# Two value products in turn instead of interleaved, and later normalizations in batch 0, in an attention and gated-MLP kernel

## The chip, the cores and the metric

The kernel runs on one core of a Trainium2 chip. The metric is the device time of one execution in microseconds (us). An execution here is about 216 us; the span in a profile is some 1.8 us shorter. Its profile shows five engines: TensorE (PE, and PEld for its weight loads), VectorE (DVE), ScalarE (ACT), GpSimd (POOL) and SyncE (SP), which here issues transfers. They run side by side (the busy times of the first four add up to 275% of the span). Each has its own queue, which it works through in order, and the traces show what it waited for. To evict a product is to copy it out of its PSUM buffer, so that the buffer is free for the next product.

## The reference, cut to what matters

```python
# attention, 4 batches x 8 heads, 768 positions, head size 64, block-sparse mask
attn = softmax(where(mask, q @ k.T / 8, -1e9)) @ v        # -> x: (4, 768, 512)
# gated MLP per batch
h = relu(x @ w_in)                     # 512 -> 1024
u, v = h[..., :512], h[..., 512:]
v_n = (v - mean(v)) / sqrt(var(v) + 1e-6)
v_s = w_spatial @ v_n + b_spatial      # mixes the 768 positions
out = (u * v_s) @ w_out
```

The MLP of one batch runs on TensorE in the gaps of the attention of the next batch. The 768 positions are six chunks of 128. For each chunk there is a value product (v0 to v5), a gate product (u0 to u5), a spatial product (s0 to s5) and an output product (o0 to o5).

## The kernel before

TensorE's queue is a chain of steps, here called slots: two score matmuls, then one to three matmuls of the MLP ("units"), then six matmuls of the attention product. A batch has 108 units: 12 products of 4, then 6 of 6, then 6 of 4. The units are a list from which each slot takes a few. Every product takes one of two alternating PSUM buffers:

```python
def bank(shape, dtype):
    moe_bank[0] = 1 - moe_bank[0]
    return psum.tile(shape, dtype, tag=f"moe{moe_bank[0]}", bufs=1, name="ps_moe")
```

so a product can start only when the product before last has been evicted. A value product is evicted on VectorE with a ReLU (L543), then its mean and variance are taken (L546, L547); after every third chunk GpSimd computes three reciprocal deviations. The normalizations (L557) are put in a queue with a due time:

```python
def v_post(tcc, ps):
    ... # ReLU into vsb, bn_stats, bn_aggr into mv
    if tcc % 3 == 2:
        ... # std, rstd on nc.gpsimd
        norm_q.extend((i, 2 * products[0] + (6 if tcc == 2 else 3)) for i in range(tcc - 2, tcc + 1))
```

`normalize_next` is called in the middle of every product with the time `2 * products[0]` (products finished so far, doubled) and after every gate product with one more; it issues at most one normalization that is due. The order of the products, and the pairs whose matmuls alternate:

```python
order = ("v0 v1 u0 v2 u1 u2 v3 v4 u3 v5 u4 u5" if b == 0 else
         "v0 v1 v2 v3 v4 v5 u0 u1 u2 u3 u4 u5" if last else
         "v0 v1 u0 v2 u1 v3 u2 v4 u3 v5 u4 u5")
for n, (w, tcc) in enumerate(order.split()):
    ... # append the four units of this product
    if n == 1 and not last or b == 0 and n == 7:
        two = units[-2 * NDM:]
        units[-2 * NDM:] = [two[i % 2 * NDM + i // 2] for i in range(2 * NDM)]
```

Interleaving two products puts off the moment at which the last quarter of `xt` (the attention output, transposed) is needed: at the seventh unit instead of the fourth.

In the experiments three more numbers matter: in which step of a head pair the casts of q, k and v on GpSimd, their transposes and the next load are issued.

```python
s_prep = {NG: 7, NG + 1: 7}.get(p, 1)                                  # casts
s_tr = {NG: 10, NG + 1: 9}.get(p, 8 if change else 6)                  # transposes
s_load = {NG: 11, NG + 1: 10, NG + 3: 10}.get(p, 9 if change else 7)   # loads
```

The softmax here doesn't subtract the row's maximum and nothing guards it: scores larger than these inputs give would overflow.

Of the kernel before, what the change touches and what calls it, by code (L numbers as in the profile page):

```python
# [26 lines left out]
def kernel(  # L27
# [469 lines left out]
    def moe_units(b):  # L497
        last = b == B - 1
# [15 lines left out]
        norm_q = deque()  # L514
        products = [0]
# [23 lines left out]
        def v_post(tcc, ps):  # L539
            if last:  # L540
                nc.scalar.activation(out=vsb[:, tcc, :], in_=ps, func=AF.Relu)  # L541
            else:
                nc.vector.tensor_scalar(out=vsb[:, tcc, :], in0=ps, scalar1=0.0,  # L543
                                        scalar2=None, op0=ALU.max)
            stats = work.tile([128, 6], FP32, tag="stats", bufs=2)
            nc.vector.bn_stats(out=stats, in_=vsb[:, tcc, :])  # L546
            nc.vector.bn_aggr(out=mv[:, tcc, :], in_=stats)  # L547
            if tcc % 3 == 2:
                cs = slice(tcc - 2, tcc + 1)
                nc.gpsimd.tensor_scalar(out=std[:, cs], in0=mv[:, cs, 1], scalar1=1e-6,  # L550
                                        scalar2=None, op0=ALU.add)
                nc.gpsimd.tensor_tensor(out=rstd[:, cs], in0=std[:, cs],
                                        in1=mhalf[:, cs], op=ALU.pow)
                norm_q.extend((i, 2 * products[0] + (6 if tcc == 2 else 3)) for i in range(tcc - 2, tcc + 1))

        def normalize(tcc):
            nc.vector.tensor_scalar(out=vn[:, tcc, :], in0=vsb[:, tcc, :],  # L557
# [12 lines left out]
        def in_proj(tcc, cols, post):  # L570
            add(NDM, lambda g: (xt(g)[:, tcc * 128:(tcc + 1) * 128], w_in_t[:, g, cols]),
                lambda ps: post(tcc, ps))
# [4 lines left out]
        for n, (w, tcc) in enumerate(order.split()):  # L577
            if w == "v":
                in_proj(int(tcc), slice(DH, DFF), v_post)
            else:  # L580
                in_proj(int(tcc), slice(0, DH), u_post)
            if n == 1 and not last or b == 0 and n == 7:
                two = units[-2 * NDM:]
                units[-2 * NDM:] = [two[i % 2 * NDM + i // 2] for i in range(2 * NDM)]

# [108 lines left out]
    for g in range(N0):  # L694
# [27 lines left out]
        if g == 26:  # L722
            moe_q.extend(moe_units(0))
# [26 lines left out]
    for p in range(NG, NP + 1):  # L750
# [6 lines left out]
        for s in range(12):  # L757
# [40 lines left out]
            if s == 11 and change:  # L798
                if p == 2 * NG:
                    for third in range(3):  # L800
                        xtr_third(p - 1, third)
                moe_q.extend(moe_units(p // NG - 1))
                slots_left = 48 if p < NP - NG else 49
                budget = 0.0
    for _ in range(len(moe_q) // 2):
        moe_q.popleft()()
    xtr(NP - 1)
    moe_q.extend(moe_units(B - 1))
    while moe_q:
        moe_q.popleft()()  # L810
# [28 lines left out]
```

## Time and profile before

| | before |
|---|---|
| time, median (range), 6 runs | 216.11 us (215.44 to 216.28) |
| span of the profiled run | 214.0 us |
| busy: TensorE, ScalarE, VectorE, GpSimd | 96%, 80%, 66%, 32% |
| slots at the places that the change touches | see the slot table under the result |

A slot's length is the distance between the starts of two successive pairs of score matmuls (L371) in TensorE's timeline. Slots are numbered g = 48, 49, ... in the order of the program; g = 48 starts the second batch's attention. In an undisturbed slot one unit makes 0.74 us, two 0.95, three 1.17. A longer slot is a stall of TensorE or holds other work as well (slot 107, 1.29, has six transposes).

### The profile page before, as it was taken

How to read it: one execution, taken by the hardware profiler on the slowest of the kernel's cores; microseconds unless marked ns; L12 is line 12 of the kernel's file. 1: busy time of each engine (PE TensorE's matmuls, PEld its weight loads, DVE VectorE, ACT ScalarE, POOL GpSimd, SP SyncE). 2: the span in 40 equal slices, each digit the busy share in tenths (PEclk: the TensorE clock that was granted, in tenths of full speed). 3: DMA queues.
4: the chain of work that ended last, by engine and by line, in shares of the span. 5: the costliest groups of instructions: out<-in, count | busy, mean ns of one | idle time of the engine just before them, and what ended most of it. 6: DMA issues, size and time to landing. Idle time of an engine off the chain costs nothing.

```text
span 214.0 us, 5304 instructions
## 1 busy us (share of the span) xinstructions
PE 206.0 (96%) x2077; PEld 126.8 (59%) x2111; DVE 141.7 (66%) x361; ACT 172.1 (80%) x238; POOL 68.8 (32%) x97
## 2 busy tenths in 40 slices
PE   8999999998999999999999999999999999999993
PEld 7667766665666666655566556555656656544441
DVE  6877949859784746366979465367869544585542
ACT  7799999998999989988899888888899885266031
POOL 6768979801440704031515310401502000022000
PEclk9999999999999999999999999999999999999999
DMA  5999999978689997999788948989902124620246
GB/s 155 305 334 381 394 349 276 213 131 254 148 225 243 282 292 131 101 308 283 258 255 118 279 89 238 229 181 284 178 1 40 25 52 86 222 101 0 58 117 242
DMA packets 64136, 42.04 MB, mean 196 GB/s; under 512 B 46096, under 2 KB 59760, under 8 KB 64112
## 3 DMA queue, kind: packets, MB, share of 16 engines
q1 hardware_dynamic: 63824, 41.39, 76.1%
q8 instruction: 16, 0.26, 0.5%
q10 hardware_dynamic: 288, 0.33, 0.5%
q14 instruction: 8, 0.07, 0.1%
HBM read 24.38 MB, written 6.29 MB: 143 GB/s over the span
## 4 chain that ended last, share of the span: by engine, by line
PE 75%; DMA 9%; issue 6%; DVE 5%; POOL 2%; SPq 1%; ACT 1%; POOLq 0%; ACTq 0%; DVEq 0%
PE ps_moe L530 29%; PE ps L371 16%; PE ps_av L387 11%; PE ps L406 5%; PE ps_t L530 3%; DMA st_q<-in_q_dram 3%; PE ps_sc L530 3%; PE ps_av L422 2%; DMA tt_q<-nat_q 2%; DMA st_k<-in_k_dram 2%; PE wps L216 2%; DMA w_spt<-ws_nat 2%; POOL vv L143 1%; DVE osb L629 1%; DVE kt_all L280 1%
## 5 line engine op out<-in xcount | busy, mean ns | idle before, releaser
L375 ACT ACTIVATE a_all<-ps 128x768 bf16<-128x768 f32 x144 | 113.3, 813 | 15.2 <-PE ps L371 8.9
L371 PE MATMUL ps<-qt_all,kt_all 88*128 88x384 bf16 x288 | 70.3, 325 | 0.0
L387 PEld LDWEIGHTS <-a_all 128*128 128x128 bf16 x864 | 46.1, 97 | 34.5 <-issue 2.1
L387 PE MATMUL ps_av<-vv,a_all 128*128 128x65 bf16 x864 | 50.8, 194 | 0.4
L530 PE MATMUL ps_moe<-w_in_t,xt 128*128 128x512 bf16 x143 | 45.1, 378 | 1.5 <-DVE vsb L543 0.9
L410 ACT ACTIVATE a_all<-ps 128x768 bf16<-128x768 f32 x48 | 35.6, 812 | 2.1 <-PE ps L406 1.5
L140 POOL CAST nat_k<-st_k 128x768 bf16<-128x768 f32 (+1 forms) x14 | 10.9, 780 | 76.4 <-DMA st_k<-in_k_dram 59.5
L530 PE MATMUL ps_moe<-vn,w_spt 128*128 128x512 bf16 x109 | 33.0, 378 | 0.5
L530 PEld LDWEIGHTS <-xt 128*128 128x128 bf16 x192 | 18.6, 97 | 14.4 <-issue 0.2
L596 DVE SCALAR_TENSOR_TENSOR gn<-ps_moe,b_col,un 128x512 bf16<-128x512 f32 x20 | 15.0, 749 | 17.7 <-PE ps_moe L530 13.1
L406 PE MATMUL ps<-qt_all,kt_all 88*128 88x384 bf16 x96 | 23.4, 325 | 0.7 <-ACT a_all L410 0.2
L530 PE MATMUL ps_moe<-w_out_t,gt 128*128 128x512 bf16 x74 | 21.5, 378 | 0.2
L530 PEld LDWEIGHTS <-w_spt 128*128 128x128 bf16 x144 | 13.8, 97 | 11.6
L371 PEld LDWEIGHTS <-kt_all 88*128 88x128 bf16 x288 | 19.1, 98 | 0.5 <-issue 0.2
L422 PEld LDWEIGHTS <-a_all 128*128 128x128 bf16 x288 | 14.9, 98 | 5.9 <-issue 0.6
L543 DVE TENSOR_SCALAR vsb<-ps_moe 128x512 bf16<-128x512 f32 x18 | 12.3, 682 | 8.7 <-PE ps_moe L530 8.7
L546 DVE BATCH_NORM_STATS2 stats<-vsb 128x6 f32<-128x512 bf16 x24 | 16.6, 694 | 1.5 <-ACT vsb L541 0.8
L422 PE MATMUL ps_av<-vv,a_all 128*128 128x65 bf16 x288 | 17.0, 194 | 0.1
L550 POOL TENSOR_SCALAR std<-mv 128x3 f32<-128x3 f32 x8 | 1.9, 242 | 41.9 <-DVE mv L547 32.6
L360 DVE COPY qt_all<-tt_q 64x384 bf16<-64x384 bf16 x48 | 14.5, 339 | 0.5
L360 DVE COPY kt_all<-tt_k 64x384 bf16<-64x384 bf16 x48 | 14.4, 338 | 0.2
L629 DVE COPY osb<-ps_moe 128x512 f32<-128x512 f32 x10 | 6.9, 689 | 11.4 <-PE ps_moe L530 7.9
(106 smaller groups left out, 218.7 us busy)
## 6 DMA issues: line engine op xcount, KB each, us to landing
out_dram<-osb SPq DMA_DIRECT2D x23, 256.0 KB, 3.0
st_v<-in_v_dram SPq DMA_DIRECT2D x14, 384.0 KB, 5.4
st_k<-in_k_dram SPq DMA_DIRECT2D x13, 384.0 KB, 4.9
st_q<-in_q_dram SPq DMA_DIRECT2D x12, 384.0 KB, 3.7
wst<-in_moe_w_spatial_dram SPq DMA_DIRECT2D x3, 768.0 KB, 9.3
wst<-in_moe_w_in_dram SPq DMA_DIRECT2D x4, 512.0 KB, 7.5
wst<-in_moe_w_out_dram SPq DMA_DIRECT2D x2, 512.0 KB, 7.5
st_q<-in_q_dram SPq DMA_DIRECT2D x4, 192.0 KB, 6.1
```

The lines of the kernel that those rows point to most:

```text
L140: eng.tensor_copy(out=dst, in_=src)
L360: nc.vector.tensor_copy(out=dst[0:D, c * 128:(c + 3) * 128], in_=src[h * D:(h + 1) * D, c:c + 3, :])
L371: nc.tensor.matmul(out=ps[:, hf * 512:hf * 512 + HALF], lhsT=kt[j % H][:, ci * 128:(ci + 1) * 128], rhs=qt[j % H][:, hf * HALF:(hf + 1) * ...
L375: nc.scalar.activation(out=a_ref[j][:, ci, :].rearrange("p (b c) -> p b c", b=2), in_=ps.rearrange("p (b c) -> p b c", b=2)[:, :, 0:HALF], ...
L387: nc.tensor.matmul(out=av_ref[j][:, qc, :], lhsT=a_ref[j][:, ci, qc * 128:(qc + 1) * 128], rhs=vv[p % NG][:, h, ci, :], start=(ci == 0), s ...
L406: nc.tensor.matmul(out=ps[:, u * 512:u * 512 + HALF], lhsT=kt[j][:, ci * 128:(ci + 1) * 128], rhs=qt[j][:, grp * HALF:(grp + 1) * HALF], s ...
L410: nc.scalar.activation(out=a_ref["half", gh][:, 2 * i:2 * i + 2, :], in_=ps.rearrange("p (b c) -> p b c", b=2)[:, :, 0:HALF], func=AF.Exp, ...
L422: nc.tensor.matmul(out=av_ref["half", gh][:, qc, :], lhsT=a_ref["half", gh][:, ci, qc * 128:(qc + 1) * 128], rhs=vv[p][:, h, ci, :], start ...
L530: nc.tensor.matmul(out=box[0], lhsT=lhs, rhs=rhs, start=(i == 0), stop=(i == n - 1))
L543: nc.vector.tensor_scalar(out=vsb[:, tcc, :], in0=ps, scalar1=0.0, scalar2=None, op0=ALU.max)
L546: nc.vector.bn_stats(out=stats, in_=vsb[:, tcc, :])
L596: nc.vector.scalar_tensor_tensor(out=gn[:, tcc, :], in0=ps, scalar=b_col[:, tcc:tcc + 1], in1=un[:, tcc, :], op0=ALU.add, op1=ALU.mult)
```

## The change

The intent: in batches 1 and 2 run v0 and v1 one after the other, so that each buffer is wanted later and left sooner; in batch 0 take the first three normalizations out of the way of the evictions of v3 and v4.

```diff
-                norm_q.extend((i, 2 * products[0] + (6 if tcc == 2 else 3)) for i in range(tcc - 2, tcc + 1))
+                norm_q.extend((i, 2 * products[0] + (3 if tcc == 5 else 12 if b == 0 else 6)) for i in range(tcc - 2, tcc + 1))
@@
-            if n == 1 and not last or b == 0 and n == 7:
+            if b == 0 and n in (1, 7):
```

Batch 0 keeps its pairs: there the last quarter of `xt` is written by the program only between the units of a pair, so one at a time would read it before it exists.

## The prediction

> **What bounds the kernel now.** I read the page's busy table first, then who TensorE waited for, then the timeline around each place that the diff touches.
>
> ```profile
> PE 206.0 (96%) x2077; PEld 126.8 (59%) x2111; DVE 141.7 (66%) x361; ACT 172.1 (80%) x238; POOL 68.8 (32%) x97
> ```
>
> TensorE is busy 96% of the 214.0 us. To see whether that is real, I listed the starts of the score matmuls (L371) from 50 to 178 us. One score step (a "slot": two score matmuls, one to three matmuls of the dense part, called units here, six of the attention product) takes 0.74 us with one unit, 0.95 with two, 1.17 with three, again and again without a gap. So TensorE sets the pace, one unit costs 0.215 us, and only slots above these times can be shortened. I found six: g=59 (1.56 for two units, 0.61 too long), g=71 (0.91 for one, 0.17), g=108 (1.29 for two, 0.34), and g=111, 156 and 159 (1.16 for two, 0.21 each). Five of the six lie at a pair of interleaved value products.
>
> ```profile
> PE ps_moe L530 <- DVE vsb L543: 0.9, 2, 0.7
> ```
>
> TensorE's own wait list holds little but this: it waits for VectorE to evict a value product (ReLU, L543) from its PSUM buffer. The two buffers of the dense part alternate, so a new product needs the one that the product before last has left.
>
> Batch 0, VectorE and then TensorE:
>
> ```profile
> 48.65 0.41 DVE L557 TENSOR_SCALAR vn<-vsb,mv,rstd 128x512 bf16<-128x512 bf16 x1
> ...
> 50.48 0.41 DVE L557 TENSOR_SCALAR vn<-vsb,mv,rstd 128x512 bf16<-128x512 bf16 x1
> 50.81 0.68 DVE L543 TENSOR_SCALAR vsb<-ps_moe 128x512 bf16<-128x512 f32 x1
> ```
>
> ```profile
> 49.98 0.38 PE L530 MATMUL ps_moe<-w_in_t,xt 128*128 128x512 bf16 x1
> ...
> 51.55 0.38 PE L530 MATMUL ps_moe<-w_in_t,xt 128*128 128x512 bf16 x1 [0.67 <-DVE vsb L543]
> ```
>
> v3 ends at about 50.36 (49.98 + 0.38), yet its eviction starts at 50.81, because two normalizations and copies queue ahead of it. u3 needs that buffer and starts at 51.55.
>
> Batch 1, all engines:
>
> ```profile
> 93.29 0.69 DVE L629 COPY osb<-ps_moe 128x512 f32<-128x512 f32 x1 [0.53 <-PE ps_moe L530]
> ...
> 93.61 0.49 PE L371 MATMUL ps<-qt_all,kt_all 88*128 88x384 bf16 x2
> ...
> 93.90 0.55 DVE L467 COPY xt<-ps_moe 128x768 bf16<-128x768 bf16 x1
> 94.03 0.84 PE L530 MATMUL ps_moe<-w_in_t,xt 128*128 128x512 bf16 x2
> ...
> 97.03 0.69 DVE L543 TENSOR_SCALAR vsb<-ps_moe 128x512 bf16<-128x512 f32 x1 [1.14 <-PE ps_moe L530]
> ...
> 97.35 0.80 PE L530 MATMUL ps_moe<-w_in_t,xt 128*128 128x512 bf16 x2
> ```
>
> Two matmuls that normally take 0.60 take 0.84: v0's first waits for the output copy (until 93.98), v1's first for the copy of xt, whose buffer it takes (until 94.45). At 97.35 (0.80) the second matmul is u0's first; it waits for v0's eviction, 97.03 to 97.72.
>
> Batch 2 has the same two, without the copy of xt:
>
> ```profile
> 142.44 0.69 DVE L629 COPY osb<-ps_moe 128x512 f32<-128x512 f32 x1 [0.99 <-PE ps_moe L530]
> ...
> 142.76 0.80 PE L530 MATMUL ps_moe<-w_in_t,xt 128*128 128x512 bf16 x2
> ...
> 145.72 0.69 DVE L543 TENSOR_SCALAR vsb<-ps_moe 128x512 bf16<-128x512 f32 x1 [1.14 <-PE ps_moe L530]
> ...
> 146.47 0.38 PE L530 MATMUL ps_moe<-w_in_t,xt 128*128 128x512 bf16 x1 [0.27 <-DVE vsb L543]
> ```
>
> **What the Trainium skill says.** "Perfetto Trace Analysis", Identifying the Most-Contended Engine, warns that TensorE's matmul busy share is no measure of headroom and points to weight-load busy time, here 59%. That is why I went by slot times. "TensorE: Matmul & The Clock Gate", Back-to-back issue gap, gives N/2.4 + 2.5 ns for one matmul alone, 216 ns at 512 columns, and about 131 ns in a stream. The trace agrees with 216 (0.215 per unit), not with 131. "VectorE: DVE Perf Modes", The perf-mode tier table, puts a bf16 tensor_scalar in SBUF in the fastest mode and one with a PSUM operand lower; the trace has 0.41 for the normalization and 0.69 for the eviction. "SBUF — State Buffer", Who interferes with whom, says that such a two-port VectorE instruction and a GpSimd instruction exclude each other for a whole instruction. The trace agrees: batch 0's fifth normalization takes 1.00 us beside the casts on GpSimd, and the sixth ends at 63.15, just after the last cast (62.12 + 0.89).
>
> ```profile
> 61.32 1.00 DVE L557 TENSOR_SCALAR vn<-vsb,mv,rstd 128x512 bf16<-128x512 bf16 x1
> ```
>
> ```profile
> 60.58 0.82 POOL L140 CAST nat_k<-st_k 128x768 bf16<-128x768 f32 x1 [1.57 <-DMA st_k<-in_k_dram]
> 61.35 0.83 POOL L140 CAST nat_q<-st_q 128x768 bf16<-128x768 f32 x1
> 62.12 0.89 POOL L143 CAST vv<-st_v 128x768 bf16<-128x768 f32 x1
> ```
>
> **The change, part by part.** No instruction is added or removed; two orders change.
>
> *Batches 1 and 2, v0 before v1.* Number the units k0, k1 and so on. Interleaved, v0 holds k0, 2, 4, 6 and v1 k1, 3, 5, 7; afterwards v0 is k0 to k3 and v1 k4 to k7. u0 is k8 either way. v1's buffer is wanted three units later, when the copies are done, so the second wait in slots 108 and 156 goes. v0 ends three units sooner, one or two slots, and its 0.69 us eviction is long done at k8, so the wait in slots 111 and 159 goes. In batch 1, v0's first matmul still waits for the output copy: 94.03 instead of 93.94 (93.61 + 0.33), so 0.09 stays of 0.34. Sum: batch 1 0.25 + 0.21 = 0.46; batch 2 0.21 + 0.21 = 0.42. All lies on TensorE's path, since ScalarE idles 0.2 to 0.4 us before most exponentials there. Sum 0.88.
>
> *Batch 0, normalizations later.* A normalization is due at twice the product number. For chunks 0 to 2 the due time goes from 2x3+6 = 12 (the seventh product, v3) to 2x3+12 = 18 (the tenth, v5). Before: chunk 0 in v3, 1 in v4, 2 in u3, 3 after u4, 4 in u5, 5 after u5. After: chunk 0 in v5, 1 in u4, 2 after u4, 3 in u5, 4 after u5, 5 in the middle of the first spatial product s0. The two ahead of v3's eviction are gone (0.33 us from start to next start each), so it can start as soon as v3 ends, near 50.39 instead of 50.81: 0.42 gained. About 0.2 of the stall remains, because the eviction itself takes 0.69.
>
> The bill comes around 62 us. Between v5's statistics and chunk 5 VectorE now does five normalizations instead of three: 2 x 0.33 more, less the 0.22 that it spent waiting for the reciprocal deviations, so 0.44 more. s0 reads the chunks in order at k51, k52 and k53 for chunks 3, 4 and 5. Moved up by 0.42, these matmuls stand at about 62.16, 62.38 and 63.1. Chunk 3 can go to VectorE at 61.03, under the first cast. If it gets the port between casts, it is done by about 61.6, chunk 4 after the second cast at 62.5, chunk 5 after the third at 63.3: 0.2 us of stall. If the casts win each time, chunk 4 is done at about 63.05: 0.7 us. So batch 0 nets between -0.2 and +0.3; I take 0.0.
>
> Sum: -0.88 + 0.0 = -0.9; 216.15 - 0.9 = 215.3 us.
>
> **The rivals.**
> - The late normalizations cost more than they save: the port lock and TensorE's want of chunk 4 speak for it, and from 61.36 eight exponentials run back to back (6.55 us), so ScalarE has no slack to give there. Against it: chunk 3 may slip between casts. Batch 0 alone would be 0.3 to 0.5 slower, total 215.7.
> - One product at a time needs the last quarter of xt at the fourth unit, not the seventh, so TensorE waits for it. In batch 1 it is copied by 94.45 and wanted after 95; in batch 2 its transpose is issued at 138.84 and lands 3.5 us later, 142.3, wanted near 143.9. Slack of 0.5 to 1.6 us speaks against it. If it failed, 0.2 to 0.5 of the gain would go.
> - ScalarE takes over as the bound (80% busy on average, nearly full in batch 0): then the 0.42 of batch 0 shrinks. Against: ScalarE idled 0.82 us in that very stall, so it moves up with TensorE. With all of batch 0's gain and none of its cost the time is 214.85.
>
> **Range and chances.** The whole bubble at these places is 0.61 + 0.34 + 3 x 0.21 = 1.58 us, 0.7% of the time, so 2% (4.3 us) is out of reach by this route; nothing in the change could cost that much either. Runs of before spread over 0.53 us, so a median of three is uncertain by some 0.2; with batch 0's uncertainty of about 0.4 the range is 214.6 to 216.0. Chances: faster by over 2% 0.01, within 2% 0.98, slower by over 2% 0.01.
>
> **What would show it right or wrong.** Right: slots 111, 156 and 159 at 0.95, slot 108 near 1.04; no wait for L543 in batches 1 and 2; slot 59 near 1.15, v3's eviction starting within 0.1 us of v3's end. The cost: a wait for L557 in the TensorE list near 62 us, with slot 72 or 73 long by 0.2 to 0.7. Wrong: a wait of TensorE for xt, slots 156 or 159 still at 1.16, or slot 72 longer by over 0.8 us.

## The result, and the profile after

The changed kernel takes 214.85 us (median of 6 runs, 214.64 to 215.09) against 216.11 us of the kernel before: 1.26 us less, inside the range, clear of the noise, and under the 2% that would count as faster. The ratio is 0.9948 with a 95% interval of 0.9931 to 0.9964. Executions over 1.5% slower than the fastest of the same kernel are left out of the means. Ratios here lie near the ratio of the means, not that of the medians quoted. The span of the profiled run fell from 214.0 to 212.8 us.

From the busy part of the page of the changed kernel, then TensorE's own list of waits:

```profile
PE 205.7 (97%) x2077; PEld 126.8 (60%) x2111; DVE 141.4 (66%) x361; ACT 172.2 (81%) x238; POOL 69.2 (33%) x97
```

```profile
PE ps_moe L530 <- DVE vsb L543: 0.3, 1, 0.3
```

The busy times are the same within 0.4 us. One wait for an eviction is left, the shortened one in batch 0. Lengths of slots in us, from the starts in the two timelines (each can be off by 0.01 from rounding); all other slots from 48 to 189 agree within 0.03:

| slot | 59 | 72 | 73 | 108 | 111 | 156 | 159 | sum of differences |
|---|---|---|---|---|---|---|---|---|
| before | 1.56 | 0.95 | 0.96 | 1.29 | 1.16 | 1.16 | 1.16 | |
| after | 1.15 | 1.06 | 1.05 | 1.04 | 0.95 | 0.96 | 0.96 | |
| difference | -0.41 | +0.11 | +0.09 | -0.25 | -0.21 | -0.20 | -0.20 | -1.07 |

Seven slots account for the whole gain in this stretch: 133.52 us from slot 48 to slot 190 after, 134.60 before.

Batch 0 after, VectorE's and TensorE's timelines around slot 59:

```profile
50.35 0.69 DVE L543 TENSOR_SCALAR vsb<-ps_moe 128x512 bf16<-128x512 f32 x1 [0.25 <-PE ps_moe L530]
```

```profile
51.09 0.38 PE L530 MATMUL ps_moe<-w_in_t,xt 128*128 128x512 bf16 x1 [0.26 <-DVE vsb L543]
```

Now VectorE waits 0.25 us for the product, instead of the product's buffer for VectorE. What is left of TensorE's wait, 0.20 us by the slot, comes from the 0.69 us of the eviction itself. (The list says 0.3, because the record of the matmul just before is missing from the trace; some others are missing too, so a pair can show as one.)

Batch 1 after, all engines, slots 108 to 111:

```profile
93.03 0.69 DVE L629 COPY osb<-ps_moe 128x512 f32<-128x512 f32 x1 [0.53 <-PE ps_moe L530]
...
93.64 0.55 DVE L467 COPY xt<-ps_moe 128x768 bf16<-128x768 bf16 x1
93.78 0.38 PE L530 MATMUL ps_moe<-w_in_t,xt 128*128 128x512 bf16 x1
...
95.36 0.69 DVE L543 TENSOR_SCALAR vsb<-ps_moe 128x512 bf16<-128x512 f32 x1
...
96.84 0.59 PE L530 MATMUL ps_moe<-w_in_t,xt 128*128 128x512 bf16 x2
```

v0's first matmul still waits for the output copy (it ends at 93.72, the matmul starts at 93.78), but nothing waits for the copy of xt. v0 is evicted from 95.36 on, and u0, whose first matmul is the second of the two from 96.84, finds its buffer free: the two take 0.59, not 0.80. Batch 2 after, all engines:

```profile
142.05 0.59 PE L530 MATMUL ps_moe<-w_in_t,xt 128*128 128x512 bf16 x2
...
143.64 0.69 DVE L543 TENSOR_SCALAR vsb<-ps_moe 128x512 bf16<-128x512 f32 x1
...
145.12 0.60 PE L530 MATMUL ps_moe<-w_in_t,xt 128*128 128x512 bf16 x2
```

Both stalls of batch 2 are gone: the stretch of 0.80 us at its start, and the wait of 0.27 us for v0's eviction. The bill of batch 0, VectorE and TensorE near 62 us (before, two normalizations stood here, not three):

```profile
60.99 2.23 DVE L557 TENSOR_SCALAR vn<-vsb,mv,rstd 128x512 bf16<-128x512 bf16 x3
```

```profile
62.12 0.71 PE L530 MATMUL ps_moe<-vn,w_spt 128*128 128x512 bf16 x2
...
63.28 0.38 PE L530 MATMUL ps_moe<-vn,w_spt 128*128 128x512 bf16 x1
```

In narrower windows the three normalizations end near 61.56, 62.39 and 63.23. The matmul of chunk 4 starts at 62.45 and that of chunk 5 at 63.28: each comes 0.05 to 0.06 us after its normalization, and slots 72 and 73 are 0.1 longer each.

### The profile page after: what moved, and what is told of

Its sections match the earlier page's. It is cut to its first block, busy times and chain, and to the rows that moved or that the text cites. A ratio compares the mean times of both kernels' runs of the same rounds, so it can differ in the third digit from the quotient of the medians.

```text
span 212.8 us, 5304 instructions
## 1 busy us (share of the span) xinstructions
PE 205.7 (97%) x2077; PEld 126.8 (60%) x2111; DVE 141.4 (66%) x361; ACT 172.2 (81%) x238; POOL 69.2 (33%) x97
## 4 chain that ended last, share of the span: by engine, by line
PE 94%; DVE 3%; issue 1%; ACT 1%; POOL 0%; ACTq 0%; DVEq 0%; POOLq 0%
PE ps_moe L530 35%; PE ps L371 22%; PE ps_av L387 13%; PE ps L406 8%; PE ps_av L422 4%; PE ps_t L530 3%; PE ps_sc L530 3%; PE wps L216 2%; DVE kt_all L280 1%; PE ps_av L443 1%; DVE vsb L543 1%; PE ps_moe L325 1%; PE ps_moe L310 0%; ACT a_all L410 0%; PE ps_moe L296 0%
```

## The experiments

The theory: TensorE is bound throughout, so each stall removed comes off the end whole, and the stalls are separate waits for single buffers. The rivals: the gain is absorbed elsewhere; interleaving itself is slow; the late normalizations cost more than they save. Twelve runs were made. All gave correct results, and all were profiled in the fast state, except the last, a single execution whose state is unknown. The first four ran on one chip, the other eight on another; the record does not name the chip of the first comparison.

One thing must be said first: in these runs the kernel before spread from 215.27 to 217.67 us (11 runs) and 215.29 to 216.88 us (8 runs), against 0.84 us in the first comparison. Verdicts on a few tenths of a microsecond therefore rest on slots, not on times.

| kernel | 59 | 72 | 73 | 108 | 111 | 124 | 130 | 156 | 159 | median us | ratio to before |
|---|---|---|---|---|---|---|---|---|---|---|---|
| before, first profile | 1.56 | 0.95 | 0.96 | 1.29 | 1.16 | 0.95 | 1.17 | 1.16 | 1.16 | 216.11 | |
| changed, first profile | 1.15 | 1.06 | 1.05 | 1.04 | 0.95 | 0.96 | 1.17 | 0.96 | 0.96 | 214.85 | 0.9948 |
| e1 orders only | 1.56 | 0.95 | 0.95 | 1.04 | 0.95 | 0.98 | 1.21 | 0.95 | 0.95 | 214.90 | 0.9948 |
| e2 normalizations only | 1.15 | 0.95 | 0.95 | 1.29 | 1.16 | 0.96 | 1.17 | 1.16 | 1.16 | 215.90 | 1.0002 |
| e3 due 10 steps after | 1.16 | 0.95 | 0.95 | 1.04 | 0.95 | 2.34 | 1.17 | 0.95 | 0.95 | 216.04 | 0.9975 |
| e4 and v3 first | 0.96 | 0.95 | 0.95 | 1.04 | 0.95 | 0.98 | 1.34 | 0.95 | 0.95 | 214.86 | 0.9942 |
| e5 second wait kept | 1.16 | 0.95 | 0.99 | 1.04 | 1.16 | 0.96 | 1.30 | 0.95 | 1.16 | 215.94 | 1.0003 |
| e6 first wait kept | 1.16 | 0.95 | 0.95 | 1.29 | 0.95 | 2.04 | 2.62 | 1.16 | 0.95 | 215.45 | 0.9995 |
| e7 load early | 1.16 | 2.07 | 0.95 | 1.04 | 0.95 | 1.00 | 2.71 | 0.95 | 0.95 | 217.02 | 1.0046 |
| e8 transfer late, changed | 1.16 | 0.95 | 0.95 | 1.04 | 0.95 | 1.97 | 1.18 | 0.95 | 0.95 | 216.46 | 1.0050 |
| e9 changed, again | 1.16 | 0.95 | 0.99 | 1.04 | 0.95 | 2.44 | 1.17 | 0.95 | 0.95 | 215.49 | 0.9963 |
| e10 deviations first | 1.16 | 0.95 | 0.95 | 1.04 | 0.95 | 0.95 | 1.17 | 0.96 | 0.95 | 214.75 | 0.9945 |
| e11 all three | 0.95 | 0.95 | 0.95 | 1.04 | 0.96 | 0.95 | 1.17 | 0.95 | 0.95 | 214.09 | 0.9921 |
| e12 transfer late, before | 1.57 | 0.95 | 0.95 | 1.29 | 1.16 | 0.95 | 1.17 | 1.16 | 1.16 | 215.74 (one run) | |

**e1, the orders alone.** The kernel before with the second hunk of the diff only.

> Batches 1 and 2 one product at a time, batch 0's normalizations as in the kernel before. Theory (every stall of TensorE removed comes off the end, nothing else moves): slots 108, 111, 156, 159 at 1.04, 0.95, 0.95, 0.95 us, slots 59, 72 and 73 as before at 1.56, 0.95 and 0.95; 0.86 us off, ratio 0.996. Rival (part of it is absorbed, by ScalarE or by a transfer): under 0.5 us off, ratio over 0.9977, and another slot grows.

All four slots came out as expected and slots 59, 72 and 73 as before. The ratio is 0.9948 (0.9912 to 0.9984). The four slots alone are 0.87 us, 0.4%; the interval holds that and more. The rival of an absorbed gain falls: no slot grew by more than 0.04 (slot 130, of which more under e9).

**e2, the normalizations alone.** The first hunk only.

> Batch 0's later normalizations alone, the order in batches 1 and 2 as before. Theory (the changed kernel's trace read slot by slot): slot 59 at 1.15, slots 72 and 73 at 1.06 and 1.05, the net is 0.21 us off, ratio 0.999; slots 108, 111, 156, 159 as before. Rival (the record's own figure for batch 0): nothing off, ratio 1.000. Rival 2 (the late normalizations cost more than they save): 0.3 to 0.5 us slower, ratio 1.0014 to 1.0023. The times alone may not part the first two; the slots do.

Slot 59 went to 1.15, but slots 72 and 73 stayed at 0.95: the cost that the changed kernel's first trace shows was not paid here. In this run the load for the casts came later, the first cast started at 61.35 instead of 60.59, and the three normalizations took 1.56 us instead of 2.23. So the 0.2 us seems to depend on when a load lands. The time, ratio 1.0002 (0.9957 to 1.0048), is too loose to tell 0.2 us from nothing.

**e3, due 10 steps after.** The changed kernel with

```diff
-... (3 if tcc == 5 else 12 if b == 0 else 6)) ...
+... (3 if tcc == 5 else 10 if b == 0 else 6)) ...
```

> The changed kernel with batch 0's first three normalizations due 10 steps after instead of 12: they then run in u3, after u3 and in v5, behind the two evictions, but all six are still before the first spatial product. Theory (slots 72 and 73 are long because chunks 4 and 5 come late): slot 59 stays at 1.15 and slots 72 and 73 go back to 0.95, 0.2 us faster than the changed kernel, ratio to the kernel before 0.9940. Rival (slots 72 and 73 are long for a shortage elsewhere, in ScalarE say): they stay at 1.05, same time as the changed kernel, ratio 0.9948.

The batch 0 slots are as the theory has them: 59 at 1.16, 72 and 73 at 0.95. After e2 that last point parts the theories less than was hoped, since e2 had 0.95 there too. The time was a surprise: 216.04 us, no better than before, with 1.39 us too many in slot 124, which no edit touches. e9 and e10 go after this.

**e4, v3 first.** e3, and the matmuls of the pair v3 and v4 in another order:

```diff
-                units[-2 * NDM:] = [two[i % 2 * NDM + i // 2] for i in range(2 * NDM)]
+                its = [iter(two[:NDM]), iter(two[NDM:])]; units[-2 * NDM:] = [next(its[a]) for a in ((0, 1) * NDM if n == 1 else (0, 0, 0, 1, 1, 0, 1, 1))]
```

> As the run before, and in batch 0 the eight matmuls of v3 and v4 in the order v3 v3 v3 v4 v4 v3 v4 v4, so that v3 ends two units sooner. Theory (what is left of the stall in slot 59 is v3's eviction itself): its eviction starts near 50.1 instead of 50.35 us, u3 waits under 0.05 us, slot 59 at 0.95 to 1.0, 0.15 to 0.2 us faster than the run before; ratio to the kernel before about 0.993, some 214.5 us. Rival (the queue of copies on VectorE holds v3's eviction back all the same): slot 59 stays at 1.15.

Slot 59 fell to 0.96: the last stall in batch 0 was the eviction itself. By the edit v3's last matmul moves from the seventh place to the sixth, one unit sooner and not two as the expectation says; two units then stand between it and u3, and they hide the eviction. TensorE's list has no wait for an eviction left. Slot 130 was 0.17 too long.

**e5 and e6, one wait at a time.** In both, batches 1 and 2 get another order of the eight matmuls of v0 and v1, batch 0 stays as changed.

```diff
+ e5: (0, 0, 0, 1, 1, 1, 0, 1)    # v1 starts late, v0 ends late
+ e6: (0, 1, 0, 0, 0, 1, 1, 1)    # v1 starts at once, v0 ends early
```

> The changed kernel, but in batches 1 and 2 the two products run in the order v0 v0 v0 v1 v1 v1 v0 v1: v1 starts three units in, v0 ends as late as in the interleaved order. Theory (two separate waits for two buffers): slots 108 and 156 short as in the changed kernel (1.04, 0.95), slots 111 and 159 long as before (1.16 each); 0.42 us slower than the changed kernel. Rival (interleaving itself slows TensorE, by switching between buffers): all four between the two kernels.

> The changed kernel, but in batches 1 and 2 the order is v0 v1 v0 v0 v0 v1 v1 v1: v1 starts at once, v0 ends two units sooner than interleaved. Theory: slots 108 and 156 long as before (1.29 and 1.16), slots 111 and 159 at 0.95; 0.46 us slower than the changed kernel. Rival as in the run before: all four between the two kernels.

TensorE's timeline, e5 at slot 111, then e6 at slots 108 and 111:

```profile
96.52 0.81 PE L530 MATMUL ps_moe<-w_in_t,xt 128*128 128x512 bf16 x2
```

```profile
93.40 0.84 PE L530 MATMUL ps_moe<-w_in_t,xt 128*128 128x512 bf16 x2
...
96.72 0.59 PE L530 MATMUL ps_moe<-w_in_t,xt 128*128 128x512 bf16 x2
```

A pair of matmuls that takes 0.59 unhindered takes 0.81 or 0.84 exactly where the edit keeps the wait. All eight slots are at one of the two values, none in between, so the two waits are separate, and interleaving as such costs nothing. The medians, 215.94 and 215.45 us, say nothing here: slots 124 and 130 swing by more.

**e7, a load issued early.** The changed kernel with `s_load` of the first pair at 9 instead of 11.

> The changed kernel with one load of q, k and v (pair 7) issued two steps earlier, ahead of two transposes, so that its three casts on GpSimd are over by about 61 us instead of 63. Theory (the last three normalizations of batch 0 wait for the port that the casts hold): they take about 0.4 us each instead of 0.57, 0.90 and 0.84, and slots 72 and 73 go back to 0.95. Rival (they are late only because five stand in a row): slots 72 and 73 stay at 1.05 whatever GpSimd does. If the load cannot move the casts, the run tells nothing.

Half an answer. The casts did move, to 58.62 to 60.99 us, and the last three normalizations, free of them, took 1.05 us together instead of 2.23, as the port theory says. (In the changed kernel's first trace they took 0.57, 0.91 and 0.91 each; the 0.90 and 0.84 of the expectation are misread.) But the load now ran ahead of the transposes of k and q, those landed late, VectorE waited 2.12 us for them, and slots 70 and 72 grew to 1.55 and 2.07. The time was 217.02 us, ratio 1.0046 (1.0001 to 1.0090); slot 130, at 2.71, has a large part in it in the profiled run. As a test of slots 72 and 73 it failed. The traces hold a cleaner one: in e6 the five normalizations stand in the order of the changed kernel and are as close together, but the first cast starts at 61.56; there the last three took 1.06 us. So it is the casts, and not the five in a row.

**e8 and e12, a late transfer under both orders.** The transposing transfer of the last quarter of `xt` for batch 2, two places later in SyncE's queue, in the changed kernel (e8) and in the kernel before (e12):

```diff
-            if s == (6 if change else 8) and p > NG and p != 2 * NG:
+            if s == 8 and p > NG and p != 2 * NG:
```

> The changed kernel with the transfer that transposes the last quarter of xt for batch 2 issued behind two others, some 2.6 us later. Theory (v0 alone wants that quarter at its fourth unit): it lands near 144 us on this kernel's clock, TensorE wants it at 143.0, and slot 157 grows by 0.5 to 1.5 us. Rival (it always lands long before): slot 157 stays at 0.95.

> The kernel before (interleaved) with the transfer of the last quarter of xt for batch 2 behind two others, as in the late-transfer run of the changed kernel, where slot 157 grew by 1.23 us. Theory (interleaved, the quarter is wanted three units later, in slot 158): slot 158 grows by at most 0.4 us and slot 157 stays at 0.95. Rival (both orders stall alike): over 1 us in slot 157 or 158.

TensorE's timeline of e8, slot 157:

```profile
145.10 0.39 PE L530 MATMUL ps_moe<-w_in_t,xt 128*128 128x512 bf16 x1 [1.06 <-DMA xt<-xn]
```

In e8 the transfer was issued at 142.2 us and landed 2.8 us later; slot 157 took 2.18 instead of 0.95. In e12, a single execution, it was issued at 142.4 and landed as fast, and slot 157 stayed at 0.95; slot 158 took 1.21 instead of 1.17. So the interleaved order hides 1.2 us of lateness that the sequential one does not. In the changed kernel as it is, the transfer is issued at 138.2 and lands by 141.5, wanted near 142.9: 1.4 us to spare.

**e9, the changed kernel again.**

> The changed kernel once more, on this call's chip, because the runs so far showed a stall that comes and goes in slots 124 and 130 of batch 1 (0.02 to 1.5 us each), where VectorE waits for GpSimd's reciprocal deviations, which stand behind casts that wait for loads. Theory: a load that lands a little later on this chip costs TensorE directly; slots 124 and 130 are long wherever VectorE's wait for the deviations exceeds about 0.7 us. Ratio to the kernel before 0.993 to 1.000, with a spread of over 1 us. Rival (the stall belongs to the experiments' edits): slots 124 and 130 at 0.95 and 1.17, spread under 0.6 us.

The six runs went from 214.53 to 218.57 us, that last one counted as slow and left out of the ratio of 0.9963 (0.9913 to 1.0014). It is counted so for its time alone; its clock was 1.00 like the others', so it may well be more of the same stall. Three runs lie at 214.5 to 214.8 us, three above 216.1. The rival falls: this is the changed kernel without an edit. The profiled run, 216.14 us, has slot 124 at 2.44. GpSimd, VectorE and TensorE of that run:

```profile
105.02 0.83 POOL L140 CAST nat_k<-st_k 128x768 bf16<-128x768 f32 x1 [7.02 <-issue]
...
106.83 0.83 POOL L143 CAST vv<-st_v 128x768 bf16<-128x768 f32 x1 [0.22 <-DMA st_v<-in_v_dram]
107.75 0.23 POOL L550 TENSOR_SCALAR std<-mv 128x3 f32<-128x3 f32 x1
108.06 0.88 POOL L552 TENSOR_TENSOR rstd<-std,mhalf 128x3 f32<-128x3 f32 x1
```

```profile
108.98 0.74 DVE L557 TENSOR_SCALAR vn<-vsb,mv,rstd 128x512 bf16<-128x512 bf16 x2 [2.15 <-POOL rstd L552]
...
110.65 0.68 DVE L543 TENSOR_SCALAR vsb<-ps_moe 128x512 bf16<-128x512 f32 x1
```

```profile
111.38 0.59 PE L530 MATMUL ps_moe<-w_in_t,xt 128*128 128x512 bf16 x2 [1.34 <-DVE vsb L543]
```

Read downwards this is one chain. The statistics of batch 1's third chunk were complete at 102.20 (L547), but the deviations stand in GpSimd's queue behind three casts, and the casts wait for loads; they start only at 107.75. (The profile names no releaser for the first cast, but its load was issued at 100.54 and landed 4.4 us later, at 104.9.) That load was itself 2.4 us later than in the first profile (98.11): it stands behind the transposes of the set before, and these behind its casts, which were late as well. Where the lateness first arose is open. VectorE stops 2.15 us for them, the eviction of v4 stands behind, and v5's first matmul waits for its buffer. The wait of VectorE and slot 124 go together over the runs: 0.38 and 0.96 (first profile), 0.40 and 0.96 (e2), 0.68 and 0.98 (e1), 1.67 and 1.97 (e8), 2.05 and 2.34 (e3), 2.15 and 2.44 (e9). About 0.65 us of it is hidden and the rest is passed on. Slot 130 has the same cause, with the second set of deviations: in e6, VectorE waited 2.32 us and slot 130 took 2.62.

**e10, the deviations first.** The changed kernel with two sets of casts moved behind them, and their transposes and loads along:

```diff
- s_prep = {NG: 7, NG + 1: 7}
+ s_prep = {NG: 7, NG + 1: 7, 2 * NG + 1: 8, 2 * NG + 2: 6}
- s_tr = {NG: 10, NG + 1: 9}
+ s_tr = {NG: 10, NG + 1: 9, 2 * NG + 1: 9, 2 * NG + 2: 8}
- s_load = {NG: 11, NG + 1: 10, NG + 3: 10}
+ s_load = {NG: 11, NG + 1: 10, NG + 3: 10, 2 * NG + 1: 10, 2 * NG + 2: 9}
```

> The changed kernel with two sets of three casts on GpSimd issued behind batch 1's two computations of the deviations instead of ahead of them (their transposes and the loads behind them move along). Theory: VectorE no longer waits for the deviations for loads, slots 124 and 130 stay at 0.95 and 1.17 in any run; it is faster than the changed kernel on the same chip by what those slots lost there (0.3 to 1.5 us), with a smaller spread; ratio to the kernel before 0.990 to 0.995. Rival (the later casts make VectorE wait for the transposes of q and k instead): other slots from 123 on grow, and the time is the same or worse.

GpSimd and VectorE of this run:

```profile
102.22 0.88 POOL L552 TENSOR_TENSOR rstd<-std,mhalf 128x3 f32<-128x3 f32 x1
103.06 0.82 POOL L140 CAST nat_k<-st_k 128x768 bf16<-128x768 f32 x1
```

```profile
106.36 0.70 DVE L557 TENSOR_SCALAR vn<-vsb,mv,rstd 128x512 bf16<-128x512 bf16 x2
```

The first set is ready 3.3 us before VectorE wants it and the second, at 114.00, 0.5 us before; VectorE waits for neither, and slots 124 and 130 are at 0.95 and 1.17. No later slot grew. The six runs lie between 214.24 and 215.25 us, median 214.75, ratio 0.9945 (0.9917 to 0.9973): a narrower spread than e9's, while a gain in time over e9 is not shown (the intervals overlap).

**e11, all three.** e10 with the batch 0 edits of e4.

> That, and the batch 0 edits of the run with v3 first (normalizations due 10 steps after, v3 ahead of v4). Theory: slot 59 at 0.95, slots 72 and 73 at 0.95, slots 124 and 130 at 0.95 and 1.17; 0.2 to 0.4 us faster than the run before on the same chip; ratio to the kernel before 0.989 to 0.994. Rival: TensorE, ahead by more, meets the next late load, and nothing is gained on the run before.

All named slots are at their undisturbed lengths, except 108 at 1.04. The six runs lie between 214.00 and 214.74 us, median 214.09, ratio 0.9921 (0.9892 to 0.9950). It is the fastest kernel by median, 0.66 us below e10. Of the 0.66 us only the 0.20 of slot 59 shows in the slots named; the rest is not explained. The intervals of the three ratios overlap, so the order of e10 and e11 is supported by their slots and by all runs but one of e11 lying at 214.32 or below, and not settled by the ratios.

## Why the prediction was right

**The bound.** That TensorE sets the pace and that slot lengths, not busy time, show where it loses any, held: the sum of seven slots, -1.07 us, is the whole difference from slot 48 to slot 190 (1.08), and in e1 four stalls removed shortened the same stretch by 0.81 us, with 0.07 lost again in slots 124 and 130.

**Batches 1 and 2.** Forecast 0.25 + 0.21 + 0.21 + 0.21 = 0.88; the slots gave 0.25 + 0.21 + 0.20 + 0.20 = 0.86, e1 alone 0.87. The predicted remainder of 0.09 in slot 108 is there (1.04). e5 and e6 show that the two waits are separate.

**Batch 0, the gain.** Forecast 0.42 with about 0.2 left; slot 59 lost 0.41, and 0.20 was left. e4 removed that as well.

**Batch 0, the bill.** This is the term that was mis-sized: "batch 0 nets between -0.2 and +0.3; I take 0.0". In the first profile the stalls measured 0.20 us and the net -0.21, at the favourable end. Of the two cases described, the one in which the third chunk gets the port between two casts took place; it ended at 61.56, 62.39 and 63.23, against 61.6, 62.5 and 63.3 forecast. For taking the middle between the cases the prediction gave no reason. The sign that it named, a wait for L557 in TensorE's list, did not appear; the two stalls of 0.1 us show only in the slots. Even this bill was not the rule: of the seven profiles with the normalizations 12 steps later (e7 aside), only the first has it whole. e2, e6 and e8, with the casts 0.8 to 1.0 us later, and e10, with them 1.4 earlier, had none; e5 and e9 had 0.04. That the casts and not the number of normalizations make the length is borne out by e6 (1.06 us for the same three, 2.23 in the first profile) and e7 (1.05).

**The rivals.** ScalarE absorbed nothing. The transfer of `xt` was in time, and e8 and e12 show what the spare time is worth. The rival that was missed is a wait. In the trace of the kernel before, VectorE does not wait for batch 1's deviations, but there is nothing to spare either, GpSimd and then VectorE:

```profile
106.56 0.88 POOL L552 TENSOR_TENSOR rstd<-std,mhalf 128x3 f32<-128x3 f32 x1
```

```profile
107.47 0.74 DVE L557 TENSOR_SCALAR vn<-vsb,mv,rstd 128x512 bf16<-128x512 bf16 x2
```

They are done at 107.44, and the normalization starts at 107.47. In the changed kernel's first trace VectorE comes to this point 0.71 us sooner (L547 just before it starts at 106.63 instead of 107.34) and the deviations only 0.29 us sooner (107.15), because they stand behind loads; VectorE waits 0.38 us, and in e9 2.15. How much of the wide spread that the kernel before also has in the experiments comes from the same chain is open: it was timed there but not profiled (its variant e12, one run, has no such wait).

**The size.** Forecast 0.9 us; the medians of the first comparison differ by 1.26, the profiled spans by 1.15, the slots by 1.07. What lies outside the slots is within what runs differ by: slot 48 alone starts anywhere from 41.5 to 42.7 us in the fourteen profiles. That the median is just the 214.85 us which the prediction gives for a batch 0 without cost is chance, since the cost was there in the slots.

## What to carry to other kernels

When an engine is saturated, measure the step length and look at the few steps that exceed it; their excess adds up to what can be gained (here the excess removed, 1.07 us, is all but 0.01 of what this stretch gained). Interleaving two accumulations makes both buffers busy longer: here it paid only where it hid a late operand (e8 and e12), so check that lateness first. Do not put a small computation that another engine waits for behind work that waits for a load in an in-order queue, since it may look free in one trace and cost 1.5 us in the next. And where no wait shows, look at how much there is to spare before moving an engine ahead: here it was 0.03 us.

## What the Trainium skill lacked or had wrong

- "TensorE: Matmul & The Clock Gate", Back-to-back issue gap: about 131 ns per 512-column matmul in a stream; every run here shows 0.215 us per unit, the value that the page gives for one matmul alone.
- "SBUF — State Buffer", Who interferes with whom: it says that whoever issues first holds the shared ports for the whole instruction, and the changed kernel's first trace agrees: the normalization from 60.99 got in before the cast of 61.36, and those from 61.49 and 62.32 waited for the casts of 61.36 and 62.20. (In the trace of the kernel before, a start of 61.32 beside one of 61.35 is too close to tell.) It does not say how this looks in a profile: the wait was inside the length of the normalizations (0.57, 0.91 and 0.91 us, against 0.41 for a free one) and not idle time before them.
- "Perfetto Trace Analysis", Identifying Dependency Chains: nothing on a chain that is slack in one execution and binding in another. Here VectorE's wait for the deviations ran from 0.38 to 2.15 us in different runs of the same kernel, and slot 124 from 0.96 to 2.44 us.
